# Routing between two mixture layers: comparisons four tiles ahead of their products, the held layer's steps moved up, and fifteen idle products

## The chip, the cores and the metric

The kernel runs on one core of one Trainium2 chip. The metric is the device time of one execution in microseconds. A core has five engines that run their own instruction queues in order: PE (matrix products), DVE (vector), ACT (activation and copies), POOL (GpSimd, which also issues the gathers and scatters) and SP (which issues the plain loads).

## The reference

The reference is an attention layer, then a mixture of 8 experts (each token goes to its best expert, in order of arrival), then a second mixture of 8 experts with a global greedy assignment. The change touches the assignment of the second one:

```python
def _moe2_ref(x, w_gate, w1, w2):
    N, D = x.shape                    # 1152, 512
    E = w_gate.shape[1]               # 8
    cap = N // E                      # 144
    logits = x @ w_gate
    flat = logits.flatten()
    order = np.argsort(-flat)         # all pairs of token and expert, best first
    assigned = -np.ones(N, dtype=np.int64)
    counts = np.zeros(E, dtype=np.int64)
    for idx in order:
        tok, e = (int(idx) // E, int(idx) % E)
        if assigned[tok] >= 0 or counts[e] >= cap:
            continue
        assigned[tok] = e
        counts[e] += 1
    ...
    for e in range(E):
        mask = assigned == e
        h = np.maximum(x[mask] @ w1[e], 0.0)      # w1: 512 x 1024
        out[mask] = h @ w2[e]                     # w2: 1024 x 512
```

## The kernel before

Everything runs in the order in which the program writes it down, engine by engine; nothing is reordered. Tokens lie in 9 tiles of 128.

**The assignment** runs in eight phases. In a phase each token names its best open expert (`Bo`, a one-hot row), and its rank is the number of tokens with the same choice and a larger logit. For that, the maxima of all tokens stand in a row on every partition (`rowb`), `compare(t)` writes `g`, 128 x 1152 ones and zeros for tile t (on DVE; for three of the nine tiles on ACT, as a sign), and `products(g, t)` adds nine products of `g` with `Bo` into one PSUM tile `pc`. Tokens of rank below 144 are placed, and at least one expert is full; its number (`evi`) is what SP needs to load that expert's weights, its token numbers (`tok`) are what POOL needs to gather its rows. The first phase covers nine tiles; the later seven cover the tokens that are left (five tiles: `pos` says where each goes, nine comparisons `cm` and 45 products move the logits there, split in three bf16 parts `S3`), and they are woven into the second mixture's experts.

**The held layer.** The last expert of the first mixture has its second layer held back as filler: `held_steps` yields 24 steps. Steps 1 to 8 and 11 to 18 are six matmuls each, 9 and 19 an ACT eviction of `y`, 10 and 20 a DVE one, 21 and 23 eight transposes, 22 and 24 an ACT copy (to `xo`, to `x2f`) and a scatter of 68 rows into `x2d`, issued by POOL. `fill()` takes the next word of the string FILL and makes as many steps as it has letters f (r: those of the expert before). The first gather of the second mixture reads `x2d`, so it waits for the last scatter.

**Weights of the second mixture** stream from memory in parts of 512 KB, four for each matrix, issued by SP in a fixed order: four of w1 and four of w2 of the first expert, then of the second, and so on. `known(p)` makes SP wait for `evi` of phase p; `quota` says how many parts may go before SP must wait for `passed(n)`, which holds it until POOL has issued the gather and then allows n more. Each w1 part passes through ACT (`wh`, the fp16 half) and DVE (`wl`, the rest).

The lines that set the order around the change:

```python
    for k, t in enumerate(tiles):          # 0 2 1 3 5 4 6 8 7
        g = compare(t)
        if k == 0:
            head(True)
        products(g, t)
        fill()
...
    quota[0] = 3
    known(0)
...
    xg = {0: gather(tok[:, 0])}
    passed(9)
```

Of the kernel before, what the change touches and what calls it, by code (L numbers as in the profile page):

```python
# [9 lines left out]
F32 = mybir.dt.float32  # L10
# [11 lines left out]
def tile_attention_moe_moe(ctx: ExitStack, tc: tile.TileContext, q, k, v, s, wg1, w1a, w2a, capacity,  # L22
                           wg2, w1b, w2b, out, dbg=None):
    nc = tc.nc
# [5 lines left out]
    P = 128  # L30
# [7 lines left out]
    NTT = NTOK // P  # L38
# [6 lines left out]
    C0, C1 = max(CAPS), min(CAPS) // 16 * 16  # L45
# [9 lines left out]
    ident = const.tile([P, P], F16, name="ident")  # L55
# [23 lines left out]
    WSP = [tuple(wsp0.tile([P, 4096], t, name=f"{n}{i}") for n, t in (("wh", F16), ("wl", BF16))) for i in range(2)]  # L79
    WS = {}  # L80

    FILL = ". rf rrrf ffff ff ffff ff ff ff . ff ff ff . . ."

# [6 lines left out]
    HELD = (E - 1,)  # L92

    ONE = (E - 2, E - 1)


    order = {}
# [5 lines left out]
    quota = [99]  # L103
# [1167 lines left out]

    fills = FILL.split()

    def fill():
        for c in fills.pop(0):
            next(todo[c], None)
# [157 lines left out]
    def slot_pe(O, R, n):  # L1434
        for t in range(n):
            nc.tensor.matmul(pt, O[:, t], R[:, t].rearrange("p e h -> p (e h)"), start=t == 0, stop=t == n - 1)
# [119 lines left out]
        nc.vector.tensor_copy(tokl, tok[:, E - 1])  # L1556


    def ranks(pc, m, Bo, Bh, n, act_t):


        order = [t for t in range(n) if t not in act_t]
        for k, t in enumerate(act_t):
            order.insert(min(3 * k + 2, len(order)), t)

        def head(first):
            for t in act_t:
                nc.tensor.matmul(pc, ones, Bh[:, t, None, :].to_broadcast([P, n, E]), start=first,
                                 stop=False, skip_group_check=True)
                nc.tensor.matmul(pc[:, t], negi, Bh[:, t], start=False, stop=False, skip_group_check=True)  # L1570
                first = False

        def compare(t):
            g = gp.tile([P, NTT, P], F16, name="g")[:, :n]
            if t in act_t:
                nc.scalar.activation(g, rowb[:, :n], AF.Sign, bias=m[:, t:t + 1], scale=-1.0)
            else:
                nc.vector.tensor_scalar(g, rowb[:, :n], m[:, t:t + 1], None, op0=OP.is_lt)
            return g

        def products(g, t):
            rhs = Bh if t in act_t else Bo
            for i in range(n):
                nc.tensor.matmul(pc[:, i], g[:, i], rhs[:, t], start=False,
                                 stop=t == order[-1] and i == n - 1, skip_group_check=True)
        return head, order, compare, products
# [23 lines left out]
    def pop_lo():  # L1610
        if late:
            split_lo(*late.pop(0))
# [12 lines left out]
    def choose(p, f):  # L1625
# [5 lines left out]
            lambda: nc.vector.reduce_sum(s2, sel.rearrange("p e h -> p h e"), axis=AX.X),  # L1631
            lambda: nc.vector.tensor_scalar(tok[:, p], s2, float(NTOK - 1), None, op0=OP.min)]

    iotac = iotat[:, :CT * P]
    m, Bo = m0, Bo0
    S3 = rp.tile([P, 3, NTT, E + 1], BF16, name="S3")
    sres = rp.tile([P, 2, NTT, E + 1], F32, name="sres")
    p0 = Banks("A2").tile([P, 512], F32)
    pc = p0[:, :NTT * E].rearrange("p (t e) -> p t e", e=E)
    head, tiles, compare, products = ranks(pc, m, Bo, Bh0, NTT, (1, 4, 7))  # L1640
    for k, t in enumerate(tiles):
        g = compare(t)
        if k == 0:
            head(True)
        products(g, t)
        fill()
    nc.gpsimd.tensor_copy(S3[:, 0], L2T)
    nc.gpsimd.tensor_sub(sres[:, 0], L2T, S3[:, 0])
    nc.gpsimd.tensor_copy(S3[:, 1], sres[:, 0])
    nc.gpsimd.tensor_sub(S3[:, 2], sres[:, 0], S3[:, 1])  # L1650
    mx = rw.tile([P, NTT], F32, name="mx0")
    nc.vector.reduce_max(mx, pc, axis=AX.X)
    BA0 = rw.tile([P, NTT, E], F16, name="BA0")
# [11 lines left out]
    f0, ops = newly_full(0)  # L1665
    O0, R0, places = slot_ones(r0, BA0, L2T[:, :, E], NTT, 0)
    in_turn(ops, places[:3])
    quota[0] = 3
    known(0)
    in_turn(places[3:])  # L1670
    pp = p0[:, 80:80 + NTT]
# [1 line left out]
    for t in range(NTT - 1):  # L1673
        nc.tensor.matmul(pp[:, t + 1:], ones, left[:, t:t + 1].to_broadcast([P, NTT - 1 - t]),
                         start=False, stop=t == NTT - 2, skip_group_check=True)
    fill()
    slot_pe(O0, R0, NTT)
    fill()
    pos = rw.tile([P, NTT], F32, name="pos")
    nc.vector.scalar_tensor_tensor(pos, pp, 1.0, left, op0=OP.add, op1=OP.mult)  # L1680
# [237 lines left out]
    FIRST, THEN = (x.split() for x in (FIRST, THEN))  # L1918
    next(work)
    pop_lo()  # L1920
    XT1[0] = spread(xg.pop(0))
    next(work)
    next(work)
# [62 lines left out]
```

## Time and profile before

| | |
|---|---|
| median of 3 runs (their range) | 463.65 us (463.37 to 463.76) |
| the profiled execution | 468.03 us |
| its span, first to last instruction | 466.2 us |
| mean granted clock of PE, share of full speed | 0.934 |
| PE busy | 402.9 us, 86% |
| DVE, ACT, POOL busy | 308.9, 249.1, 189.9 us |
| moved by DMA | 103.02 MB, mean 221 GB/s |

The profile is one execution; all points in time ("at 292.40") are microseconds from the start of its span. Its own time is 1.8 us over its span, and 4.4 us over the median of the runs, so what the trace shows of waits need not hold to the microsecond in the other executions.

### The profile page before, as it was taken

Reading aid. Unit: us, or ns where it says so; the run is one execution under the profiler, and the core shown is the slowest. Engines: PE = TensorE matmul, PEld = TensorE weight load, DVE = VectorE, ACT = ScalarE, POOL = GpSimd, SP = SyncE. Lnnn points to the kernel's source line nnn. Section 1 sums busy time; section 2 is a strip of 40 time slices with the busy share of each in tenths; the row PEclk is TensorE's granted clock in tenths of the full one; section 3 lists DMA queues with packets and bytes.
Section 4 is the critical chain, followed back from the end, with each engine's and each line's share of the span. In section 5 each row is a group of like instructions: output and inputs, shape, how many; then the busy total and the mean of one; then the engine's idle time right before and its main releaser. Section 6 shows DMA issues by size and latency. Waiting matters only on the chain. (4 is left out here: it accounts for less than half of the span.)

```text
span 466.2 us, 13648 instructions
## 1 busy us (share of the span) xinstructions
PE 402.9 (86%) x5245; PEld 376.6 (81%) x5245; DVE 308.9 (66%) x926; ACT 249.1 (53%) x459; POOL 189.9 (41%) x306
## 2 busy tenths in 40 slices
PE   2679999978979979999999996469989999999970
PEld 1457888867768969999999996459979999999970
DVE  6879999887585557777888944757754664555100
ACT  4447888845752545555668434242746465465320
POOL 4487888858804220410441811422331342342110
PEclk9869999989999998999999989559989999999995
DMA  6797999849834799999996900479996869798000
GB/s 158 173 199 165 215 223 215 190 155 321 265 101 180 200 353 400 346 353 321 296 348 118 167 7 23 160 200 307 364 376 208 284 224 318 255 286 290 29 20 25
DMA packets 94398, 103.02 MB, mean 221 GB/s; under 512 B 56136, under 2 KB 63304, under 8 KB 94323
## 3 DMA queue, kind: packets, MB, share of 16 engines
q1 hardware_dynamic: 88931, 91.85, 68.1%
q0 software_dynamic: 4192, 9.91, 7.0%
q8 instruction: 43, 0.70, 0.6%
q10 hardware_dynamic: 1200, 0.30, 0.3%
q14 instruction: 32, 0.26, 0.2%
HBM read 81.42 MB, written 14.59 MB: 206 GB/s over the span
## 5 line engine op out<-in xcount | busy, mean ns | idle before, releaser
L162 DVE TENSOR_TENSOR wl<-wf,wh 128x1024 bf16<-128x1024 f32 x64 | 77.7, 1234 | 23.3 <-ACT wh L158 23.1
L158 ACT ACTIVATE wh<-wf 128x1024 f16<-128x1024 f32 x64 | 65.7, 1050 | 19.6 <-DMA wf<-in_moe_w_dram 19.6
L986 PE MATMUL C<-h,wf 128*128 128x160 f32 (+7 forms) x544 | 60.3, 273 | 2.2 <-ACT h L940 2.2
L929 PE MATMUL A<-xt,wh 128*128 128x144 f16 (+4 forms) x288 | 60.9, 235 | 0.0
L930 PE MATMUL A<-xt,wh 128*128 128x144 f16 (+4 forms) x288 | 60.9, 235 | 0.0
L931 PE MATMUL A<-xt,wl 128*128 128x144 f16 (+4 forms) x288 | 60.8, 235 | 0.0
L1099 POOL DMA_INDIRECT x2d<-xo,tix x14 | 22.9, 1637 | 86.4 <-DVE l L1095 34.7
L930 PEld LDWEIGHTS <-wh 128*128 128x128 f16 x512 | 51.3, 100 | 1.1 <-issue 0.6
L931 PEld LDWEIGHTS <-wl 128*128 128x128 bf16 x512 | 51.5, 101 | 0.4 <-DVE wl L162 0.4
L929 PEld LDWEIGHTS <-wh 128*128 128x128 f16 x512 | 51.4, 100 | 0.2 <-issue 0.2
L534 ACT ACTIVATE pf<-pE,XB 128x512 f32<-128x512 f32 (+4 forms) x80 | 36.8, 514 | 10.1 <-PE pE L529 9.8
L1860 POOL DMA_INDIRECT out_dram<-x2f,tok x14 | 15.5, 1108 | 64.8 <-ACT h L940 37.3
L986 PEld LDWEIGHTS C<-h,wf 128*128 128x128 f32 x256 | 37.2, 195 | 2.5 <-ACT h L940 2.5
L1840 PE MATMUL C<-h,wf 128*128 128x144 f32 x256 | 37.0, 298 | 2.2 <-ACT h L940 2.2
L412 POOL TENSOR_TENSOR pl<-pf,ph 128x512 f16<-128x512 f32 x30 | 35.5, 1193 | 6.2 <-DVE ph L401 4.0
L486 DVE CUSTOM_DVE_ANT_0 junk<-pM,cb 128x128 f16<-128x128 f32 (+4 forms) x80 | 32.1, 430 | 6.9 <-PE pM L476 6.2
L1840 PEld LDWEIGHTS C<-h,wf 128*128 128x128 f32 x256 | 34.0, 198 | 2.4 <-ACT h L940 2.4
L474 PE MATMUL pM<-al,ar 128*128 128x128 f16 (+2 forms) x96 | 27.8, 328 | 7.0 <-DVE rm L486 7.0
L1441 POOL DMA_INDIRECT xg<-x2d,tok x16 | 22.7, 1418 | 23.6 <-PE C L1840 6.8
L557 PE MATMUL pog<-vf,pf 128*128 128x65 f32 x180 | 28.7, 282 | 0.0
L931 PE MATMUL C<-xt,wl 128*128 128x144 f16 x128 | 25.6, 232 | 0.3 <-DVE wl L162 0.3
L929 PE MATMUL C<-xt,wh 128*128 128x144 f16 x128 | 25.7, 232 | 0.0
(408 smaller groups left out, 1164.9 us busy)
## 6 DMA issues: line engine op xcount, KB each, us to landing
wf<-in_moe_w_dram SPq DMA_DIRECT2D x128, 512.0 KB, 8.7
xd<-zero SPq DMA_DIRECT2D x18, 257.0 KB, 4.7
cb<-cumd SPq DMA_DIRECT2D x16, 288.0 KB, 4.8
x2d<-zero SPq DMA_DIRECT2D x9, 260.5 KB, 4.5
kf<-in_k_dram SPq DMA_DIRECT2D x16, 128.0 KB, 3.7
vf<-in_v_dram SPq DMA_DIRECT2D x16, 128.0 KB, 3.0
qf<-in_q_dram SPq DMA_DIRECT2D x14, 128.0 KB, 2.9
bl<-al SPq DMA_DIRECT2D x16, 72.0 KB, 4.9
```

What stands on the lines that cost most here:

```text
L158: nc.scalar.activation(hi, src, AF.Copy)
L162: nc.vector.tensor_sub(lo, src, hi)
L412: (nc.gpsimd if ENG[name][i % 2] == "P" else nc.vector).tensor_sub(o, x, y)
L474: nc.tensor.matmul(o, AR[m][:, t * P:(t + 1) * P], AL[m][:, j0:j1], start=True, stop=not diag)
L486: nc.vector.tensor_tensor_reduce(junk[:w, :j1 - j0], o, CB[m][:w, j0:j1], 1.0, r if t == 4 and j0 == 0 else -3e38, OP.add, OP.max, r)
L534: nc.scalar.activation(d, o, AF.Exp, bias=x, scale=2.0 ** -13)
L557: nc.tensor.matmul(o, pf[:, c:c + P], VF[n % 4][:, j, h], start=False, stop=j == t)
L929: nc.tensor.matmul(ph[:, g], wh[:, c, fs], xt[:, c], start=c == 0, stop=False)
L930: nc.tensor.matmul(ph[:, g], wh[:, c, fs], xt[:, 4 + c], start=False, stop=False)
L931: nc.tensor.matmul(ph[:, g], wl[:, c, fs], xt[:, c], start=False, stop=c == 3)
L986: nc.tensor.matmul(py[:, g], a[:, f, d], b[:, f], start=k == 0, stop=k == len(terms) - 1)
L1840: nc.tensor.matmul(py[:, g], a[:, f, d], b[:, f], start=k == 0, stop=k == len(terms) - 1)
```

## The change

It makes five edits. (1) In the first phase the comparisons of four tiles stand ahead of the first product, and each later one ahead of the products four tiles before it; the tiles come in the order 0 1 2 4 3 7 5 6 8, so that ACT and DVE take turns. (2) FILL has other words: the held matmuls come within the first three tiles, the second scatter after the eighth. (3) The three-part split of the logits (`S3`, four POOL instructions) stands ahead of the first phase's products instead of behind them. (4) `quota` is 2, not 3. (5) `warm(n)` issues n products of 128 x 512 into a spare bank whose result nobody reads: 6 after the counts of phase 0, 5 after the products with `O0`, 4 ahead of the first `spread`.

```diff
-    FILL = ". rf rrrf ffff ff ffff ff ff ff . ff ff ff . . ."
+    FILL = ". rf rrrf ffff ffffff ffff ffff . . ff ff . . . . ."
+    WARM2 = (6, 5, 4)
...
-    def ranks(pc, m, Bo, Bh, n, act_t):
+    def ranks(pc, m, Bo, Bh, n, act_t, apart=3):
...
-            order.insert(min(3 * k + 2, len(order)), t)
+            order.insert(min(apart * k + apart - 1, len(order)), t)
...
+    def warm(n):
+
+        o = Banks("C1").tile([P, 512], F32)
+        for _ in range(n):
+            nc.tensor.matmul(o, ident, iotat[:, :512], start=True, stop=True)
...
-    head, tiles, compare, products = ranks(pc, m, Bo, Bh0, NTT, (1, 4, 7))
-    for k, t in enumerate(tiles):
-        g = compare(t)
-        if k == 0:
-            head(True)
-        products(g, t)
-        fill()
+    head, tiles, compare, products = ranks(pc, m, Bo, Bh0, NTT, (1, 4, 7), 2)
     nc.gpsimd.tensor_copy(S3[:, 0], L2T)
     nc.gpsimd.tensor_sub(sres[:, 0], L2T, S3[:, 0])
     nc.gpsimd.tensor_copy(S3[:, 1], sres[:, 0])
     nc.gpsimd.tensor_sub(S3[:, 2], sres[:, 0], S3[:, 1])
+    AHEAD = 4
+    gs_ = [compare(t) for t in tiles[:AHEAD]]
+    head(True)
+    for k, t in enumerate(tiles):
+        if k + AHEAD < NTT:
+            gs_.append(compare(tiles[k + AHEAD]))
+        products(gs_[k], t)
+        fill()
...
-    quota[0] = 3
+    quota[0] = 2
...
     fill()
+    warm(WARM2[0])
     slot_pe(O0, R0, NTT)
+    warm(WARM2[1])
     fill()
...
     pop_lo()
+    warm(WARM2[2])
     XT1[0] = spread(xg.pop(0))
```

On DVE, in the first phase, from the first comparison to the maximum over the finished counts (`g` comparisons, `y` the two evictions of the held layer, `mx` the maximum), the rows before:

```order
L1578 TENSOR_SCALAR g<-rowb,m_3109 128x1152 x2
L1253 SCALAR_TENSOR_TENSOR y<-C_5152,y 128x2x136
L1578 TENSOR_SCALAR g<-rowb,m_3109 128x1152 x3
L1253 SCALAR_TENSOR_TENSOR y<-C_5321,y 128x2x136
L1578 TENSOR_SCALAR g<-rowb,m_3109 128x1152
L1652 TENSOR_REDUCE mx_5485<-A_5278 128x9
```

and now:

```order
L1580 TENSOR_SCALAR g<-rowb,m_3109 128x1152 x3
L1255 SCALAR_TENSOR_TENSOR y<-C_5152,y 128x2x136
L1580 TENSOR_SCALAR g<-rowb,m_3109 128x1152
L1255 SCALAR_TENSOR_TENSOR y<-C_5322,y 128x2x136
L1580 TENSOR_SCALAR g<-rowb,m_3109 128x1152 x2
L1662 TENSOR_REDUCE mx_5485<-A_5278 128x9
```

Both evictions stay, one comparison moved ahead of the first and one behind the second.

On POOL, from the last held scatters to the first gather (`S` and `sres` the logits' parts, `xo` and `x2f` the rows of the two scatters), before:

```order
L1099 DMA x2d<-xo,tix 1152x521
L1268 MEMSET x2f 68x8
L1098 TENSOR_SCALAR x2f<-gs 68x1
L1099 DMA x2d<-x2f,tix 1152x521
L1647 CAST S_5276<-L2T 128x81
L1648 TENSOR_TENSOR sres<-L2T,S_5276 128x81
L1649 CAST S_5276<-sres 128x81
L1650 TENSOR_TENSOR S_5276<-sres,S_5276 128x81
L1441 DMA xg<-x2d,tok 72x521 x2
```

and now:

```order
L1649 CAST S_5276<-L2T 128x81
L1650 TENSOR_TENSOR sres<-L2T,S_5276 128x81
L1651 CAST S_5276<-sres 128x81
L1652 TENSOR_TENSOR S_5276<-sres,S_5276 128x81
L1270 MEMSET xo 68x8
L1100 TENSOR_SCALAR xo<-gs 68x1
L1101 DMA x2d<-xo,tix 1152x521
L1270 MEMSET x2f 68x8
L1100 TENSOR_SCALAR x2f<-gs 68x1
L1101 DMA x2d<-x2f,tix 1152x521
L1443 DMA xg<-x2d,tok 72x521 x2
```

The four rows of the parts went from behind the scatters to ahead of them; the gather now follows the second scatter directly.

On SP, where the first expert's w1 is loaded (`evi` the wait for its number, `wf_78` the buffer, `gone` the wait for the gather), before:

```order
L1615 TENSOR_LOAD evi
L1615 ISA x2
L126 ISA
L126 DMA wf_78<-in_moe_w_dram 128x4x256
L126 ISA
L126 DMA wf_78<-in_moe_w_dram 128x4x256
L126 ISA
L126 DMA wf_78<-in_moe_w_dram 128x4x256
L1621 TENSOR_LOAD gone
L1621 ISA x2
L126 ISA
L126 DMA wf_78<-in_moe_w_dram 128x4x256
```

and now:

```order
L1617 TENSOR_LOAD evi
L1617 ISA x2
L128 ISA
L128 DMA wf_78<-in_moe_w_dram 128x4x256
L128 ISA
L128 DMA wf_78<-in_moe_w_dram 128x4x256
L1623 TENSOR_LOAD gone
L1623 ISA x2
L128 ISA
L128 DMA wf_78<-in_moe_w_dram 128x4x256
L128 ISA
L128 DMA wf_78<-in_moe_w_dram 128x4x256
```

The third part went behind the wait for the gather. Since `passed` still allows nine parts, the last part of the second expert's w1 went behind the next such wait in the same way.

## Rows read from the trace of the kernel before

**Rows 1.** Stages: us, busy us of PE, PEld, DVE, ACT, POOL; clock; DMA; GB/s.

```profile
293.00:302.00 9.00, 3.37 (x75) 3.00 (x73) 6.92 (x37) 2.08 (x2) 3.77 (x6) 0.50 0.61 196
320.00:340.00 20.00, 19.69 (x277) 19.42 (x276) 14.47 (x63) 10.09 (x18) 5.97 (x9) 1.00 1.03 339
340.00:344.00 4.00, 1.85 (x15) 1.62 (x14) 2.12 (x8) 2.96 (x5) 0.73 (x1) 0.88 1.05 394
```

**Rows 2.** POOL in time: start, length, operation, idle time before it and its releaser.

```profile
291.66 1.14 POOL L1099 DMA_INDIRECT x2d<-xo,tix  x1 [9.62 <-ACT xo L1267]
295.22 1.13 POOL L1099 DMA_INDIRECT x2d<-x2f,tix  x1 [2.09 <-DVE R L1422]
...
297.16 1.54 POOL L1649 CAST S<-sres 128x81 bf16<-128x81 f32 x1
...
302.94 1.54 POOL L1441 DMA_INDIRECT xg<-x2d,tok  x1 [3.83 <-DVE Bh L1728]
```

**Rows 3.** Issue to landing, us, of the two scatters at 291.66 and 295.22.

```profile
x2d<-xo,tix POOLq DMA_INDIRECT x1, 4.4
x2d<-x2f,tix POOLq DMA_INDIRECT x1, 6.8
```

**Rows 4.** DVE in time, from the first comparison to the logits' move.

```profile
280.42 1.55 DVE L1578 TENSOR_SCALAR g<-rowb,m 128x1152 f16<-128x1152 f32 x2 [1.38 <-ACT rowb L1146]
...
287.58 0.44 DVE L1253 SCALAR_TENSOR_TENSOR y<-C,y 128x272 f16<-128x272 f32 x1 [2.08 <-ACT y L1251]
...
292.40 0.23 DVE L1652 TENSOR_REDUCE mx<-A 128x9 f32<-128x72 f32 x1 [3.65 <-PE A L1584]
...
294.09 0.15 DVE L1596 TENSOR_SCALAR evi<-evf 128x1 int32<-128x1 f32 x1
...
296.72 0.17 DVE L1632 TENSOR_SCALAR tok<-s 72x2 int32<-72x2 f32 x1
...
297.03 1.55 DVE L1696 TENSOR_SCALAR g<-iotat,pos 128x640 bf16<-128x640 f16 x5
```

**Rows 5.** PE in time: held matmuls, one tile's products, and the second mixture's first.

```profile
281.54 0.87 PE L1247 MATMUL C<-h,wf 128*128 128x136 f16 x12
282.25 0.37 PE L1584 MATMUL A<-Bo,g 128*128 128x8 f16 x9
282.48 0.87 PE L1247 MATMUL C<-h,wf 128*128 128x136 f16 x12
...
309.21 0.28 PE L929 MATMUL D<-xt,wh 128*128 128x144 f16 x1 [0.49 <-ACT xt L1464]
```

**Rows 6.** ACT in time: the second eviction of `y`, and the copy ahead of the first scatter.

```profile
287.15 0.40 ACT L1251 ACTIVATE y<-C 128x272 f16<-128x272 f32 x1 [1.92 <-PE C L1247]
...
289.74 1.02 ACT L1267 ACTIVATE xo<-D 68x1024 f16<-68x1024 f16 x1 [2.20 <-PE D L1265]
```

**Rows 7.** SP's queue in time: issues of weight parts, each of 512 KB.

```profile
295.32 0.40 SPq L126 DMA_DIRECT2D wf<-in_moe_w_dram  x1
...
306.75 0.38 SPq L126 DMA_DIRECT2D wf<-in_moe_w_dram  x1
...
317.23 0.33 SPq L126 DMA_DIRECT2D wf<-in_moe_w_dram  x1
```

**Rows 8.** DVE and PE in the first expert's first layer.

```profile
315.25 2.35 DVE L162 TENSOR_TENSOR wl<-wf,wh 128x1024 bf16<-128x1024 f32 x2
...
316.53 0.24 PE L931 MATMUL C<-xt,wl 128*128 128x144 f16 x1 [0.26 <-DVE wl L162]
```

**Rows 9.** ACT and PE in the second expert, where weights are waited for.

```profile
326.20 1.06 ACT L158 ACTIVATE wh<-wf 128x1024 f16<-128x1024 f32 x1 [4.92 <-DMA wf<-in_moe_w_dram]
330.30 0.23 PE L929 MATMUL C<-xt,wh 128*128 128x144 f16 x1
...
341.05 1.06 ACT L158 ACTIVATE wh<-wf 128x1024 f16<-128x1024 f32 x1 [4.36 <-DMA wf<-in_moe_w_dram]
342.45 0.79 PE L1840 MATMUL C<-h,wf 128*128 128x144 f32 x4 [2.15 <-ACT h L940]
```

## The prediction

> **What bounds the kernel now.** I read the stages first. Over most of the span PE is full, as from 320 to 340, where it works 19.69 of 20 us [rows 1]; only around the first routing phase it is empty, with 3.37 us of work in the 9 us from 293 to 302 at half the clock (0.50 granted, that is 1.2 GHz). So I followed what releases what from the first comparison to the second mixture's first matmul at 309.21 [rows 5]. The weights come next, since DMA is full from 320 to 340 (share 1.03, 339 GB/s) [rows 1].
>
> The chain, back from 309.21: the rows of the first expert come from a gather that POOL issues at 302.94 [rows 2], 6.27 us before the first matmul. Its token numbers had been there since 296.72 + 0.17 = 296.89 [rows 4]. What it waited for is the last held scatter, since it reads the same buffer: issued at 295.22 [rows 2], landed after 6.8 us [rows 3], at 302.02; POOL goes on 0.92 later. (The trace names a DVE instruction as releaser; a scatter's landing fits, and the program has POOL wait for it.) The first scatter landed in 4.4 us; the second shared the memory with three weight parts that SP began to issue at 295.32 [rows 3, 7]. So the first 6 us after `tok` are the price of a late scatter, not of routing.
>
> Why is it late? The scatter's rows come from the held layer, which stands between the tiles' products. DVE does the second eviction of `y` at 287.58, having done one comparison after another ahead of it, and the last tiles' products wait for comparisons again: `mx`, which needs them all, starts at 292.40 after 3.65 us of idleness on DVE [rows 4].
>
> **The change, part by part.** *Comparisons ahead, held layer early.* From 281.54 on PE does, by the new order, two more tiles' products and the 60 held matmuls that are left before it needs an eviction. Twelve held matmuls take 0.71 us (281.54 to 282.25) and a tile's products 0.23 (282.25 to 282.48) [rows 5]: 5 x 0.71 + 2 x 0.23 = 4.0, so 285.6. The comparisons don't hold this up: DVE needs 0.78 each [rows 4], starts at 280.42, and has three done by 282.8, while ACT makes tiles 1 and 4. ACT's eviction follows in 0.2 and takes 0.40, DVE's begins 0.43 after ACT's begins (287.15 and 287.58) and takes 0.44 [rows 4, 6]: done at 286.7. Eight transposes, 0.45 by the twelve above, and ACT copies `xo` from 287.1 to 288.1; now it starts at 289.74 [rows 6]. POOL's scatter began 0.90 after that copy's end (290.76 to 291.66) [rows 2, 6], so the first is issued at 289.0. The second copy follows without a gap (1.02 more), and POOL is busy 1.14 with the first scatter and some 0.8 (my allowance) with two small instructions: 290.1 if nothing but the copy counts, 291.0 with POOL; I take 291.0, 4.2 earlier than 295.22. The last two comparisons follow the eviction on DVE: 286.7 + 2 x 0.78 = 288.2, a last product 0.23, so `mx` at 288.5, 3.9 earlier.
>
> *S3 ahead.* These four run on POOL while it waits for `xo`. One of them took 1.54 [rows 2] and they stood between scatter and gather, but the gather waited longer than that, so moving them alone is worth nothing. They do release the 45 products of the logits' move earlier, which no longer reach 302.
>
> *The scatter's landing.* SP's issue follows `evi` by 1.23 (294.09 to 295.32) [rows 4, 7]; both move with `mx`, so the first part is issued at 291.4, right after the scatter as now, but two parts instead of three. The landing lies between the 4.4 of the undisturbed scatter and the 6.8 of the disturbed one: 295.4 to 297.8. I take 6.0, since two thirds of the disturbance are there for as long as the scatter runs: 297.0, and the gather at 297.9. Earlier by 5.0; bounds 4.2 and 6.6.
>
> *Gather to first matmul:* 6.27 as before, so 304.2, 5.0 earlier. POOL may be slowed there. The Trainium skill, "SBUF — State Buffer", section "Who interferes with whom", says that a vector instruction in a two-port mode blocks GpSimd for its whole length, descriptor generation included. The trace agrees for POOL's arithmetic: the cast of 1.54 us at 297.16 lasted as long as five comparisons of 1.55 at 297.03 [rows 2, 4]. By that rule a gather among such comparisons would lose up to 1.5 us. In my sum the nine comparisons are over by then (they start 3.9 earlier, or 2.9 if the idle products run slow), so I charge nothing and keep 1.5 for the range.
>
> *Idle products.* The six stand in a wait of PE for DVE, the five in front of the logits' move, the four in front of the transposes that wait for the gather. No trace row shows one; 512 columns against the 136 of a held matmul (0.71 / 12 = 0.059 us) give 0.22 us each, 0.44 at half clock: 1.3 to 2.7, 1.1 to 2.2 and 0.9 to 1.8 us. `tok` may be late by 1 us through the first, and still precedes the landing by 3. So they cost nothing as long as the scatter ends last. Do they give anything? A faster PE in the first expert's layer 1 doesn't: the third quarter's `wl` is the first of two splits of 2.35 us that begin at 315.25, 6 us after the first matmul, and DVE is busy throughout; PE already waits 0.26 for it at 316.53 [rows 8]. I take 0.
>
> *Quota 2.* One more part comes behind the gather. The stream proper now begins at 306.75 [rows 7], 3.81 after the gather; it will begin at 301.7, 5.0 earlier, with 0.52 MB more to bring: 1.6 us at 339 GB/s [rows 1]. Also the second expert's last w1 part goes behind the second gather; now it is issued at 317.23 [rows 7], then at about 317 (12.9 us after the first matmul, where the next parts are issued now): the stream has just run dry there, some 0.4 us lost.
>
> *What is late next.* In the second expert PE waits 2.15 us at 342.45, because ACT stands 4.36 us at 341.05 for the third expert's w1 and has an eviction of `h` queued behind it [rows 9]. This wait ends by the stream. The stream gains 5.0 - 1.6 - 0.4 = 3.0, PE 5.0: so PE waits 4.1 there and leaves 3.0 us earlier. Behind it PE is full to the end, and everything shifts.
>
> The sum: 468.03 - 3.0 = 465.0 against the profiled execution; carried over as a difference, 463.65 - 3.0 = 460.6. That the profiled execution is 4.4 above the median leaves open whether the stream is as tight in the others; part of the wait may be missing there, which gives up to 2 us more. I take 460.3.
>
> **The rivals.** *The whole gain arrives.* The stream keeps up (no or a shorter wait at 342.45 in unprofiled runs), or the scatter lands undisturbed (gather 6.6 earlier, of which the stream leaves 4.6): 463.65 - 4.6 or - 5.0, so 458.6 to 459.0, both together 457. For it: the 4.4 us between profile and median, and two parts instead of three. Against it: DMA at a share of 1.03.
>
> *The scatter is hardly faster, or the gather is blocked.* 4.2 - 1.6 - 0.4 = 2.2, less up to 1.5 for the blocked gather: 461.4 to 463.0. For it: the parts still go out within half a microsecond of the scatter.
>
> *The clock.* By rows, PE's clock was 0.88 over the 4 us with that 2.15 us wait, so it fell behind it [rows 1, 9]. If the idle products lift the clock for layer 1, its first half ends in about half of the 7.3 us from 309.21 to 316.53 [rows 5, 8], and PE stands some 3.6 us for `wl`, with a fall behind it that costs 1 to 2 us. That is an estimate; PE is 2.0 ahead of the stream, which takes up most of it: 460.3 to 461. The Trainium skill, "TensorE: Matmul & The Clock Gate", section "Why this matters for your kernels", says that idle gaps between bursts send the clock back to 1.2 GHz. By that rule the edit would fill one gap and open another; the trace agrees with the fall, and the time would stay as above.
>
> *Slower: the part behind the second gather.* Now ACT gets the second expert's w1 at 326.20 and PE needs it at 330.30; hi and lo splits take 1.06 and 1.2, so 1.8 us are spare [rows 9]. The part issued at 317.23 took 9.0 to 326.2. Issued at 317 it decides once it needs over 11.1 us; at 13, 466 or so. Against it: less is queued ahead of it than now, so I expect 5 to 6.
>
> **How the numbers follow.** My forecast (459.2 to 461.4) gets 0.5, the whole gain (below 459.2) 0.27, the small one (461.4 to 463.0, with some beyond) 0.18, slower 0.05. A measurement of this kernel can tell 0.2%, 0.93 us. Of the small gain a third lies within it, and of the slower case a little: faster 0.88, same 0.08, slower 0.04. The range takes in the whole gain down to 457.6 and the small one up to 462.7.
>
> **What would show it.** `mx` 3.9 us earlier than 292.40; the second scatter near 291 and its landing in about 6 us; the gather near 298, first matmul near 304; a wait of PE in the second expert of 3 to 4 us instead of 2.15. It would be wrong if the gather stayed near 302, if the idle products stood between `tok` and anything that ends last, or if w1 of the second expert came after 328.

## The result and the profile after

The changed kernel takes 456.39 us (median of 4 runs, 455.61 to 464.24) against 463.51 us of the kernel before beside it (4 runs, 461.79 to 463.76): a ratio of 0.9849, 95% interval 0.9815 to 0.9882. Now and then a run falls into a slower state, here the one of 464.24; such runs count in the medians, but not in the ratios, here and below. That is 7.1 us less. The forecast was 460.3, which is 3.35 less than the 463.65 that it started from, and 456.39 lies below the range's 457.6.

| | before | after |
|---|---|---|
| the profiled execution, us | 468.03 | 456.74 |
| its span, us | 466.2 | 454.7 |
| mean granted clock | 0.934 | 0.970 |

The two profiled executions are 11.5 us of span apart, and not all of it is the change's. The first tile's products, the first work that the change moves, start at 281.30 before and at 276.78 after: 4.52 us lie ahead of the change. In unchanged code from 20 to 30 us the granted clock was 0.50 before and 0.72 after, from 260 to 280 it was 0.91 and 1.00. So from here on points in time count from the first tile's products, written as +x. The offset is 281.30 for the groups of rows of before, 276.78 for the rows below.

| us behind the first products | before | after | earlier by | forecast |
|---|---|---|---|---|
| `mx` | +11.10 | +7.23 | 3.9 | 3.9 |
| second held scatter issued | +13.92 | +9.50 | 4.4 | 4.2 |
| gather issued | +21.64 | +16.03 | 5.6 | 5.0 |
| first matmul of the second mixture | +27.91 | +21.80 | 6.1 | 5.0 |
| SP's first weight part behind the second gather | +40.84 | +34.74 | 6.1 | 5.0 |
| ACT gets the third expert's w1 | +59.75 | +54.35 | 5.4 | 3.0 |
| PE's wait in the second expert ends | +61.15 | +55.76 | 5.4 | 3.0 |
| end of the span | +184.9 | +177.9 | 7.0 | 3.0 |

PE of the changed kernel in time (start, length, operation, idle time before it and its releaser), to be read against [rows 5, 9]:

```profile
276.78 0.38 PE L1586 MATMUL A<-Bo,g 128*128 128x8 f16 x9
277.01 1.58 PE L1249 MATMUL C<-h,wf 128*128 128x136 f16 x24
...
285.06 1.45 PE L1640 MATMUL C<-iotat,ident 128*128 128x512 f16 x6
...
287.57 1.24 PE L1640 MATMUL C<-iotat,ident 128*128 128x512 f16 x5
288.94 2.66 PE L1710 MATMUL A<-S,g 128*128 128x27 bf16 x45
...
293.06 1.03 PE L1640 MATMUL C<-iotat,ident 128*128 128x512 f16 x4
...
298.58 0.28 PE L931 MATMUL D<-xt,wh 128*128 128x144 f16 x1 [0.49 <-ACT xt L1466]
...
332.54 0.76 PE L1852 MATMUL C<-h,wf 128*128 128x144 f32 x4 [1.97 <-ACT h L942]
```

The held matmuls are done in bursts of 24, 24 and 12, and among the nine tiles' products PE stands for a comparison only once, 0.27 us. Before, it stood three times, and the eight transposes that each scatter needs come behind such a product:

```profile
284.13 0.38 PE L1584 MATMUL A<-Bh,g 128*128 128x8 f16 x9 [0.79 <-ACT g L1576]
...
288.80 0.38 PE L1584 MATMUL A<-Bo,g 128*128 128x8 f16 x9 [1.26 <-DVE g L1578]
289.04 0.61 PE L1265 MATMUL D<-ident,y 128*68 128x128 f16 x8
291.96 0.40 PE L1584 MATMUL A<-Bh,g 128*128 128x8 f16 x9 [2.30 <-ACT g L1576]
292.22 1.05 PE L1265 MATMUL D<-ident,y 128*68 128x128 f16 x8
```

```profile
290.66 1.24 ACT L1576 ACTIVATE g<-rowb,m 128x1152 f16<-128x1152 f32 x1
```

The longest of these waits, 2.30 us, is for ACT's last comparison, which stood behind ACT's copy of `xo` at 289.74 [rows 6].

The fifteen idle products (line 1640) take 1.45, 1.24 and 1.03 us, 0.24 to 0.26 each where the estimate was 0.22, and end 4.5 us ahead of the matmul at 298.58. The wait in the second expert is 1.97 us, not the 4.1 forecast.

DVE in time, against [rows 4]:

```profile
275.90 2.28 DVE L1580 TENSOR_SCALAR g<-rowb,m 128x1152 f16<-128x1152 f32 x3 [1.38 <-ACT rowb L1148]
...
281.64 0.44 DVE L1255 SCALAR_TENSOR_TENSOR y<-C,y 128x272 f16<-128x272 f32 x1 [1.86 <-ACT y L1253]
282.00 1.54 DVE L1580 TENSOR_SCALAR g<-rowb,m 128x1152 f16<-128x1152 f32 x2
284.01 0.23 DVE L1662 TENSOR_REDUCE mx<-A 128x9 f32<-128x72 f32 x1 [0.47 <-PE A L1586]
...
286.02 0.82 DVE L1430 TENSOR_TENSOR O<-iota0f,hq 128x648 f16<-128x648 f32 x1
...
288.51 2.74 DVE L1708 TENSOR_SCALAR g<-iotat,pos 128x640 bf16<-128x640 f16 x9
```

Three comparisons stand ahead of everything, two behind the second `y`, and DVE is idle 0.47 us ahead of `mx`, where it was 3.65. The nine comparisons of the logits' move end at 291.25.

POOL in time, against [rows 2], and behind it issue to landing of the two scatters, against [rows 3]:

```profile
284.45 1.18 POOL L1101 DMA_INDIRECT x2d<-xo,tix  x1 [4.57 <-ACT x2f L1269]
...
286.28 1.55 POOL L1101 DMA_INDIRECT x2d<-x2f,tix  x1 [0.31 <-POOL x2f L1100]
292.81 1.06 POOL L1443 DMA_INDIRECT xg<-x2d,tok  x1 [4.98 <-DVE Bo L1739]
294.18 1.02 POOL L1443 DMA_INDIRECT xg<-x2d,tok  x1 [0.30 <-issue]
```

```profile
x2d<-xo,tix POOLq DMA_INDIRECT x1, 4.4
x2d<-x2f,tix POOLq DMA_INDIRECT x1, 5.7
```

The second scatter lands at 286.28 + 5.7 = 291.98, and the gather follows 0.83 later: the same wait as before, shorter by an earlier start and by 1.1 us of landing. The first gather takes 1.06 us where it took 1.54.

ACT in time, against [rows 9]:

```profile
316.81 1.06 ACT L160 ACTIVATE wh<-wf 128x1024 f16<-128x1024 f32 x1 [6.15 <-DMA wf<-in_moe_w_dram]
...
331.13 1.06 ACT L160 ACTIVATE wh<-wf 128x1024 f16<-128x1024 f32 x1 [4.17 <-DMA wf<-in_moe_w_dram]
```

Stages of the changed kernel, columns as in [rows 1]: first the stretch that answers to 293 to 302, then the first expert's first layer, then the wait in the second expert, which was at 340 to 344:

```profile
288.50:297.50 9.00, 5.18 (x66) 3.12 (x65) 5.36 (x21) 2.77 (x4) 2.32 (x5) 1.00 0.56 165
297.50:304.50 7.00, 6.51 (x87) 6.40 (x88) 6.27 (x30) 4.50 (x6) 0.49 (x2) 0.52 1.10 321
330.00:334.00 4.00, 2.04 (x20) 1.81 (x19) 2.44 (x11) 2.87 (x5) 0.64 (x1) 1.00 1.04 381
332.00:336.00 4.00, 3.46 (x31) 3.45 (x32) 3.64 (x7) 3.40 (x7) 1.80 (x2) 1.00 1.05 399
```

The clock is 1.00 through the first stretch (0.50 before, at rows 1's 293 to 302), but the first layer runs at 0.52 again, since PE stands for the gather first. Around the wait it stays 1.00; before it was 0.88, and 0.69 in the four us behind:

```profile
309.00:316.00 7.00, 6.79 (x89) 6.78 (x89) 6.79 (x31) 4.02 (x6) 0.48 (x2) 0.52 1.11 307
344.00:348.00 4.00, 4.00 (x25) 4.00 (x25) 2.61 (x5) 1.75 (x4) 2.77 (x3) 0.69 1.02 379
```

These two stages are of the kernel before: its first layer at 0.52 too, and the fall behind its wait.

### The profile page after: what moved, and what is told of

It is laid out like the page before. It is cut to its first block, busy times and chain, and to the rows that moved or that the text cites. A ratio compares the mean times of both kernels' runs of the same rounds, so it can differ in the third digit from the quotient of the medians.

```text
span 454.7 us, 13676 instructions
## 1 busy us (share of the span) xinstructions
PE 400.4 (88%) x5260; PEld 371.6 (82%) x5260; DVE 309.2 (68%) x926; ACT 249.1 (55%) x459; POOL 190.9 (42%) x306
## 5 line engine op out<-in xcount | busy, mean ns | idle before, releaser
L988 PE MATMUL C<-h,wf 128*128 128x160 f32 (+7 forms) x544 | 58.6, 269 | 1.7 <-ACT h L942 1.7
L933 PE MATMUL A<-xt,wl 128*128 128x144 f16 (+4 forms) x288 | 59.5, 231 | 0.0
L931 PE MATMUL A<-xt,wh 128*128 128x144 f16 (+4 forms) x288 | 59.5, 231 | 0.0
L932 PE MATMUL A<-xt,wh 128*128 128x144 f16 (+4 forms) x288 | 59.5, 231 | 0.0
L1101 POOL DMA_INDIRECT x2d<-xo,tix x14 | 23.0, 1640 | 78.0 <-DVE l L1097 40.2
L932 PEld LDWEIGHTS <-wh 128*128 128x128 f16 x512 | 50.7, 99 | 1.1 <-issue 0.6
L931 PEld LDWEIGHTS <-wh 128*128 128x128 f16 x512 | 50.8, 99 | 0.2 <-issue 0.2
L988 PEld LDWEIGHTS C<-h,wf 128*128 128x128 f32 x256 | 36.2, 190 | 1.9 <-ACT h L942 1.9
L1852 PE MATMUL C<-h,wf 128*128 128x144 f32 x256 | 35.5, 290 | 2.0 <-ACT h L942 2.0
L1852 PEld LDWEIGHTS C<-h,wf 128*128 128x128 f32 x256 | 32.5, 190 | 2.2 <-ACT h L942 2.2
```

Of the source, the lines that this page charges most:

```text
L931: nc.tensor.matmul(ph[:, g], wh[:, c, fs], xt[:, c], start=c == 0, stop=False)
L932: nc.tensor.matmul(ph[:, g], wh[:, c, fs], xt[:, 4 + c], start=False, stop=False)
L933: nc.tensor.matmul(ph[:, g], wl[:, c, fs], xt[:, c], start=False, stop=c == 3)
L988: nc.tensor.matmul(py[:, g], a[:, f, d], b[:, f], start=k == 0, stop=k == len(terms) - 1)
L1852: nc.tensor.matmul(py[:, g], a[:, f, d], b[:, f], start=k == 0, stop=k == len(terms) - 1)
```

## The experiments

Each was timed in rounds beside the kernel before on the same chip. Ratios are to that, with the 95% interval. The points behind the first products are from each run's trace; "end" is the end of the span. The last column is SP's first weight part behind the second gather, of which more below.

| run | median us (before) | ratio | second scatter | gather | first matmul | third w1 at ACT | end | SP |
|---|---|---|---|---|---|---|---|---|
| e5_order_only | 460.54 (466.59) | 0.9864 [0.982, 0.9908] | +9.48 | +16.10 | +22.00 | +52.8 | +176.5 | +34.9 |
| e3_old_order | 463.5 (464.39) | 0.9977 [0.9947, 1.0007] | +14.02 | +21.47 | +27.24 | +59.3 | +182.9 | +40.2 |
| e6_idle_only | 466.69 (466.59) | 0.9992 [0.9954, 1.0031] | +13.93 | +21.36 | +27.42 | +57.7 | +182.6 | +40.3 |
| e1_no_idle | 457.45 (464.39) | 0.9847 [0.9799, 0.9896] | +9.50 | +16.07 | +21.78 | +52.8 | +176.3 | +34.7 |
| e4_quota2_only | 464.56 (464.39) | 1.0043 [1.0003, 1.0084] | +13.92 | +21.39 | +27.85 | +57.6 | +182.2 | +40.8 |
| e2_quota3 | 457.61 (464.39) | 0.9861 [0.9812, 0.9911] | +9.51 | +16.12 | +21.72 | +52.1 | +175.7 | +34.6 |
| e8_passed10 | 460.92 (466.59) | 0.989 [0.9843, 0.9937] | +9.51 | +16.06 | +21.63 | +52.0 | +176.9 | +34.5 |
| e7_quota0 | 468.05 (466.59) | 1.0014 [0.9983, 1.0044] | +9.50 | +15.10 | +26.62 | +58.2 | +183.7 | +39.6 |
| e17_quota1 | 462.37 (463.16) | 0.9987 [0.9958, 1.0016] | +9.51 | +15.89 | +26.83 | +58.0 | +181.5 | +39.8 |
| e10_ahead_oldfill | 460.44 (465.09) | 0.9914 [0.9886, 0.9943] | +10.58 | +17.21 | +22.83 | +53.1 | +176.7 | +35.8 |
| e16_ahead_oldfill | 459.67 (463.16) | 0.9932 [0.9902, 0.9961] | +10.69 | +17.49 | +23.14 | +54.3 | +177.9 | +36.1 |
| e11_fill_only | 463.88 (465.09) | 0.9978 [0.9954, 1.0001] | +12.84 | +17.97 | +25.82 | +56.7 | +180.4 | +38.8 |
| e12_before_less | 465.48 (465.09) | 0.9993 [0.9969, 1.0018] | +13.93 | +21.28 | +27.88 | +58.0 | +181.7 | +40.8 |
| e13_after_less | 460.65 (465.09) | 0.9926 [0.9899, 0.9953] | +9.51 | +15.96 | +21.59 | +52.3 | +177.1 | +34.5 |
| e15_after_less | 458.1 (463.16) | 0.9869 [0.982, 0.9919] | +9.50 | +15.99 | +21.56 | +53.0 | +178.2 | +34.5 |
| e14_change | 458.78 (463.16) | 0.9899 [0.9858, 0.994] | +9.50 | +16.06 | +21.70 | +53.5 | +177.0 | +34.7 |

**Which edits bring it.** The kernel before with the new order of comparisons, products and held steps alone (edits 1 and 2; the logits' parts stay behind, `quota` stays 3, no idle products):

```diff
-    FILL = ". rf rrrf ffff ff ffff ff ff ff . ff ff ff . . ."
+    FILL = ". rf rrrf ffff ffffff ffff ffff . . ff ff . . . . ."
...
-    for k, t in enumerate(tiles):
-        g = compare(t)
-        if k == 0:
-            head(True)
-        products(g, t)
+    gs_ = [compare(t) for t in tiles[:AHEAD]]
+    head(True)
+    for k, t in enumerate(tiles):
+        if k + AHEAD < NTT:
+            gs_.append(compare(tiles[k + AHEAD]))
+        products(gs_[k], t)
```

> The kernel before with the new order of the first phase alone (comparisons four ahead, tile order, fill string): three weight parts, the split of the logits behind the loop, no idle products. Theory A: within 0.3% of the whole change, 456 to 458 us. If quota, split and idle products matter together: 459 to 461.

It measured 0.9864, with the same points behind the first products as the whole change. Its counterpart is the changed kernel with that piece turned back:

> The change with the tile loop and the fill string of before; the split of the logits ahead, two parts and the idle products stay. Theory A: nearly the whole gain is gone, 461 to 463 us, since the second scatter is issued near 295 again. Theory B or C: most of the gain stays, 457 to 459.

0.9977, an interval that takes in no change, and the points of the kernel before. The idle products alone in the kernel before (e6: `warm` and its three calls as in the change), and the changed kernel without them (e1):

```diff
-    WARM2 = (6, 5, 4)
+    WARM2 = (0, 0, 0)
```

> The kernel before with the fifteen idle products alone. Theory A: no change, 463 to 465 us, since each stands in a wait. Theory B: 1.5 to 2 us faster, 462 to 463, with the clock at full speed in the logits' move and behind the second expert's wait.

> The change without its fifteen idle products, all else kept. Theory A (the gain comes through the earlier scatter and gather alone): 456 to 457 us, within 0.2% of the whole change; the gather comes 4.5 to 5 us before that of the kernel before, counted from the first tile's products. Theory B (the idle products hold the clock up, and this saves time in the routing and behind the second expert's wait): 1.5 to 2.5 us slower than the change, 458 to 459, and the clock at half in the stretch of the logits' move.

0.9992 and 0.9847: they give and cost nothing that these intervals can show. So edits 1 and 2 bring the gain, and what the other three add can't be told from nothing.

**How it splits between them.** The changed kernel with the old words of FILL, once, and once more beside the changed kernel itself on another chip; then the kernel before with the new words alone (e11, the same line the other way round):

```diff
-    FILL = ". rf rrrf ffff ffffff ffff ffff . . ff ff . . . . ."
+    FILL = ". rf rrrf ffff ff ffff ff ff ff . ff ff ff . . ."
```

> The changed kernel with the old words of FILL: the comparisons stand four tiles ahead, the held layer stays spread over the tiles. If the comparisons carry the gain, PE reaches the second eviction after about 60 x 0.059 + 7 x 0.23 = 5.1 us from its first products, the last scatter follows within 0.6 us of the 9.50 that the whole change has, and the time is within 1 us of it (ratio 0.985 to 0.988 to the kernel before). If the held layer's words carry it, the scatter stays behind 12 us and the ratio is above 0.993.

> The changed kernel with the old words of FILL, beside the changed kernel. Its trace had the first matmul of the second mixture 1.0 us later behind the first products (22.8 against 21.8), so if that instant decides the time, it is 1.0 us above the changed kernel beside it; if the two edits only work together, 3 us or more.

> The kernel before with the new words of FILL alone: the held layer comes within the first three tiles, the comparisons stand where they stood. The eviction of y on DVE then comes ahead of some five comparisons, so I expect the maximum over the counts some 9 us behind the first products (11.10 before, 7.23 with the whole change) and the last scatter near 10.5 us. If the held layer's words carry the gain, the ratio is near 0.988; if the comparisons do, or if both are needed, it is above 0.993.

The comparisons ahead without the new words came to 0.9914, between the 0.988 that the first expectation allowed if they carried all and the 0.993 of the other, and to 0.9932, just above that. The scatter came at +10.58 and +10.69, 1.1 to 1.2 us behind that of the whole change, and not within 0.6. In e16 the time is 0.9 us above the changed kernel beside it by the medians (459.67 against 458.78), 1.5 by the ratios (0.9932 against 0.9899), where the first matmul is 1.4 us later; the intervals overlap. The words alone came to 0.9978, an interval that takes in no change. So the comparisons carry most of the gain, about two thirds to four fifths in e16, and the words give the rest only together with them. My numbers for the words alone were wrong: `mx` came at +12.71, not +9, and the scatter at +12.84, not +10.5. POOL and DVE of e11_fill_only:

```profile
301.08 3.03 POOL L1441 DMA_INDIRECT xg<-x2d,tok  x1 [2.00 <-DVE g L1696]
304.41 1.05 POOL L1441 DMA_INDIRECT xg<-x2d,tok  x1 [0.30 <-issue]
```

```profile
289.13 0.44 DVE L1253 SCALAR_TENSOR_TENSOR y<-C,y 128x272 f16<-128x272 f32 x1 [3.28 <-ACT y L1251]
289.49 3.00 DVE L1578 TENSOR_SCALAR g<-rowb,m 128x1152 f16<-128x1152 f32 x4
...
300.41 2.74 DVE L1696 TENSOR_SCALAR g<-iotat,pos 128x640 bf16<-128x640 f16 x9
```

With the held layer early and no comparisons ahead, DVE stands 3.28 us in front of `y` with four comparisons queued behind it. And since the routing is later too (`tok` is ready at 300.43), the gather at 301.08 falls into the nine comparisons and takes 3.03 us instead of 1.06. That is the rival of the blocked gather, here in full: 2 us. The Trainium skill, "SBUF — State Buffer", section "Who interferes with whom", says that a DVE instruction in a two-port mode shuts GpSimd out for its whole length; this row agrees, with 2.0 us more beside 2.74 us of comparisons.

**Parts ahead of the gather.** `quota` 2 in the kernel before (e4); 3 in the changed kernel (e2); and ten parts instead of nine behind the first gather in the changed kernel (e8), which puts the last part of the second expert's w1 ahead of the second gather again:

```diff
e4
-    quota[0] = 3
+    quota[0] = 2
e2
-    quota[0] = 2
+    quota[0] = 3
e8
-    passed(9)
+    passed(10)
```

> The kernel before with two weight parts ahead of the gather instead of three, nothing else. Theory C: the scatter lands 1 us sooner, gather 1 us sooner, 462 to 463 us. The prediction's term for the stream: 1 to 2 us slower than before, 464.5 to 465.5.

> The change with three weight parts ahead of the gather, as before, instead of two. Theory C (two parts disturb the scatter less, and the later part costs nothing): the scatter takes 6.5 to 7 us to land instead of 5.7, and the time is 0.8 to 1.2 us longer than the change, 457.3. The prediction's own term (the extra part behind the gather costs the weight stream 1.6 to 2.0 us): 0.5 to 1.5 us faster than the change, 455 to 456.

> The change with ten instead of nine parts allowed behind the first gather, so that the second expert's last w1 part is issued with its three others again. If its delay costs anything (the prediction charged 0.4 us): 0.4 us faster than the change, 456.0; if not, the same within what can be told.

With the new order `quota` 3 (0.9861) and 2 (0.9849) can't be told apart, nor 0.989 with ten parts; alone, 2 was 0.4% slower, just outside no change. The part moved behind the second gather costs no time that can be told. Then none and one part ahead of the gather in the changed kernel:

```diff
e7
-    quota[0] = 2
+    quota[0] = 0
...
-    passed(9)
+    passed(11)
e17
-    quota[0] = 2
+    quota[0] = 1
...
-    passed(9)
+    passed(10)
```

> The change with no weight part ahead of the gather, and eleven instead of nine allowed behind it, so that the later waits stand where they stood. Theory C's mechanism by itself: the scatter lands undisturbed after 3.3 to 4.4 us and the gather comes 1.3 to 2.4 us sooner. The prediction's term for the stream: two parts of 1.6 us later, against that 1.3 to 2.4 sooner, so 1 to 2 us slower than the change at the second expert's wait, 457.5 to 458.5; if the stream is not what ends there, 454.5 to 456.

> The changed kernel with one weight part ahead of the gather and ten behind it. If parts in flight slow the scatter's landing (5.7 us behind two of them, 4.4 undisturbed), the gather is issued some 0.5 us earlier behind the first products (15.5 instead of 16.0), and the first matmul with it, if its second to fourth parts come in time: 0.5 us less, too little to be told. If the first expert's own weights are late, as with none ahead, the time rises by 2 us or more.

Both lose nearly all the gain. With none, the gather comes at +15.10, 0.9 earlier; with one, at +15.89, hardly. But the first matmul comes at +26.6 and +26.8. ACT of e17_quota1, and PE's transposes of the gathered rows:

```profile
302.00 1.06 ACT L160 ACTIVATE wh<-wf 128x1024 f16<-128x1024 f32 x1 [6.28 <-DMA wf<-in_moe_w_dram]
302.96 0.75 ACT L1148 ACTIVATE rowb<-A 128x384 f32<-128x384 f32 x2
304.44 0.64 ACT L1466 COPY xt<-A 128x576 f16<-128x576 f16 x1 [0.73 <-PE A L1463]
```

```profile
303.49 1.15 PE L1463 MATMUL A<-ident,xg 72*128 72x72 f16 x16 [7.87 <-ACT rowb L1148]
```

ACT's queue has the splits of two weight parts ahead of its copies to `rowb`; PE's transposes wait for these, and `xt`, which PE needs for its first matmul, is copied behind the transposes. The second part, issued behind the gather, arrives at 302.00, and all of this waits for it. So 2 is the least that this order of ACT's queue allows, and with a third nothing changes that can be told.

**Is the weight stream a limit?** The four loads of the first expert's second matrix (2.1 MB) left out, in the kernel before (e12) and in the changed one (e13, and e15 once more):

```diff
-        nc.sync.dma_start(t[sl], src[sl])
+        if i != 2 * E + 1:
+            nc.sync.dma_start(t[sl], src[sl])
```

> The kernel before without the loads of the first expert's second matrix in the second mixture (its four parts, 2.1 MB; that expert then multiplies with what the buffer held, so its rows are not the reference's). At 339 GB/s the stream behind it comes some 6 us earlier. If the stream sets the end in the second expert, as the prediction had it, the wait of 2.15 us there goes, with the fall of the clock behind it: 2 to 4 us less than before. If the stream is no limit, under 1 us.

> The changed kernel with the same loads left out. By the prediction PE waits 4.1 us for the stream there, so it would gain 4 us or more over the changed kernel, more than the kernel before gains, and stand 5 us or more below it with the loads left out. If the stream is no limit in either, both gain under 1 us, and the two without these loads differ by the same 6 to 7 us as the two with them.

The first moved nothing: 0.9993, interval 0.9969 to 1.0018, where 2 to 4 us less would have been 0.991 to 0.996. The second stood at 0.9926, 4.8 us below the first, which neither theory had quite, and without the changed kernel on its chip. So both were timed together, with the changed kernel unaltered:

> The changed kernel once more, unaltered, on the chip on which the next three are timed, since the two runs with a matrix left out were timed where the change itself was not. 0.985 to 0.990 to the kernel before.

> The changed kernel without the loads of the first expert's second matrix in the second mixture (its rows are then not the reference's). If PE waits for the weight stream in the changed kernel's second expert, as the prediction had it, 3 to 4 us below the changed kernel beside it; if the stream is no limit, the same within 1 us.

458.78 and 458.10: without 2.1 MB 0.7 us less by the medians and 1.4 by the ratios (0.9899 and 0.9869), with overlapping intervals. That lies between the two expectations and by itself decides nothing. The kernel before does decide, and so do the traces: without these loads PE still waits in the second expert, 1.02 us in e13 and 1.80 in e15, against 1.97 and 0.71 with them (the changed kernel's two traces). These bytes are no limit, though ACT still waits for weights. ACT of e15_after_less, and what SP's queue waited for from 313 to 318 (total, times, longest):

```profile
335.60 1.06 ACT L161 ACTIVATE wh<-wf 128x1024 f16<-128x1024 f32 x1 [4.00 <-DMA wf<-in_moe_w_dram]
```

```profile
SPq L1624 <- POOL gone L1623: 4.3, 1, 4.3
```

The third expert's w1 comes at 335.60 - 282.56 = +53.0 (+52.3 in e13) against +53.5 with all loads, where the bytes left out are worth 2.1 MB / 339 GB/s = 6.2 us [rows 1]. What takes these 6.2 us up is a stop: SP stands for the second gather, and the third expert's w1 is issued behind it. The same wait in the kernel before (320 to 322) and in the changed one (309 to 312), each with the issue behind it:

```profile
SPq L1621 <- POOL gone L1620: 3.8, 1, 3.8
322.14 0.39 SPq L126 DMA_DIRECT2D wf<-in_moe_w_dram  x1
```

```profile
SPq L1623 <- POOL gone L1622: 3.7, 1, 3.7
311.52 0.34 SPq L128 DMA_DIRECT2D wf<-in_moe_w_dram  x1
```

322.14 is 12.93 us behind the first matmul at 309.21, and 311.52 is 12.94 behind 298.58. In all eighteen traces, with the old order or the new, none to three parts ahead of the first gather, and the 2.1 MB loaded or not, that distance is 12.86 to 12.95 us, while the wait itself is 2.4 to 4.3 us long. What comes behind the stop was not varied: up to the last part of the third expert's w1 SP issues eight parts there, nine in the changed kernel, in stages whose DMA share is 1.05 [rows 1] and 1.04. No run left out any of these.

## Why the prediction was wrong

**What held.** The chain did: the gather waits for the second held scatter. In e3 and e16 the trace names that scatter's landing as the releaser. POOL of e16_ahead_oldfill:

```profile
296.55 1.06 POOL L1443 DMA_INDIRECT xg<-x2d,tok  x1 [5.68 <-DMA x2d<-x2f,tix]
```

`mx` came 3.9 us earlier as forecast, the scatter 4.4 (4.2). The logits' parts and the idle products were costed at nothing, and e5_order_only is 0.9864 without either. The gather was not blocked, as the nine comparisons were over by then. The reading of why the scatter was late was half right: DVE, whose row of comparisons the prediction names first, was idle for 2.08 us ahead of its eviction [rows 4]. It was PE that stood for comparisons, longest for the last one on ACT.

**Small terms.** The landing took 5.7 us, not 6.0, but not for the reason given, so that 6.0 was near is luck. The prediction counted on two parts disturbing the scatter less than three. With the first part issued 0.1 us behind the scatter, two parts gave 6.6 us (e3, e4) and three 6.8 (before); in the new order the gather came at +16.12 with three (e2) and at +16.03 to +16.07 with two. What changed is that the first part went out 1.5 us behind the scatter at 286.28, and not 0.4:

```profile
287.75 0.40 SPq L128 DMA_DIRECT2D wf<-in_moe_w_dram  x1
```

With one part ahead the gather came only 0.1 to 0.2 us earlier than with two or three, with none 0.9 to 1.0. Gather to first matmul shrank from 6.27 to 5.77: the first gather took 1.06 us instead of 1.54, since in the old order it meets a `wl` split of DVE (the last section has the rows). So the first matmul came 6.1 earlier in this pair of traces instead of 5.0. In the other executions of the old order with all loads (e3, e4, e6: +27.24 to +27.85) against the new with the same words and at least two parts (+21.63 to +22.00) it is 5.2 to 6.2.

**The step that failed** is "What is late next": "The stream gains 5.0 - 1.6 - 0.4 = 3.0, PE 5.0: so PE waits 4.1 there and leaves 3.0 us earlier." I had the stream run from the first gather on at 339 GB/s, so that one more part behind that gather shifts everything behind it. It doesn't: SP stops at the second gather, for 3.7 us in the trace after and 4.3 with 2.1 MB less to bring. The third expert's w1 is issued behind that stop, and the stop ends 12.9 us behind the first matmul, so it moves with PE. The prediction had this distance (it wrote "12.9 us after the first matmul, where the next parts are issued now") and counted it as 0.4 us lost rather than as the place from which the stream starts again. Of the extra part's 1.6 us, now ahead of the third w1, 0.7 were left in this pair: ACT's wait ends 54.35 - 34.74 = 19.6 us behind the stop, 18.9 before. In the other traces with all loads this distance is 16.8 to 19.2 us with two parts ahead of the first gather and 17.3 to 17.9 with three, so even the 0.7 can't be told from what executions differ by. PE's wait ends 5.4 us earlier, not 3.0, and it is 1.97 us long, not 4.1.

**The wait itself** was no property of the order. Old order: 2.15 us in the trace of before, 1.0 in e3, 0.6 in e6, none to be seen in e4. New order: 2.0, 1.1 (e5), 0.7 (e2), 0.7 (e14), none to be seen in e1 and e8. I built on one execution, 4.4 us above the median, in which the clock fell behind that wait (0.88, then 0.69). Two traces of the new order have the same fall, e7 behind a wait of 1.84 us and e15 behind 1.80, and the changed kernel has none behind 1.97. The four us that begin 1.5 us behind the wait, in e7, e15 and the changed kernel:

```profile
345.30:349.30 4.00, 4.00 (x26) 4.00 (x24) 2.74 (x6) 1.76 (x4) 2.65 (x3) 0.70 1.04 407
```

```profile
338.50:342.50 4.00, 4.00 (x24) 4.00 (x23) 2.53 (x5) 1.73 (x4) 2.85 (x3) 0.66 1.03 406
```

```profile
334.00:338.00 4.00, 4.00 (x39) 3.98 (x38) 2.56 (x5) 2.09 (x5) 2.85 (x3) 1.00 1.03 404
```

From the end of this wait to the end of the span it is 123.8 to 124.1 us in the three traces with the fall. In the others that wait there it is 122.1 to 122.3, but for e6 and e13 (123.5 and 123.3), where PE waits once more, 1.3 and 1.0 us. So the fall accounts for the last 1.6 us of the 7.0 in the pair of traces, and it goes with the execution and not with the order.

The ends of the spans of e3, e4 and e6 are +182.2 to +182.9, mean 182.6; those of the changed kernel, e14, e1, e2, e5 and e8 are +175.7 to +177.9, mean 176.7. So 5.8 us is what the order gives from the first products on (6.4 with the trace of before counted too), about what the first matmul gains. From the first matmul to the end of the span it is 153.8 to 157.0 us in all eighteen traces, with the old order (153.8 to 157.0) as with the new (153.9 to 157.0): within that spread nothing behind the first matmul takes the gain back. The medians of these kernels, each against the kernel before on its chip, lie 4.4 to 7.1 us lower. The 7.1 of the first comparison is at the upper end of that; what is between them may be in part the clock in code ahead of the change, where the first products start anywhere from 276.8 to 285.7 us. How much is that was not measured by itself.

**The rivals.** "The whole gain arrives", at 0.27, came nearest, by its first half: the first matmul's gain passes through whole. Its ground, that the stream keeps up, was not quite what happened, since ACT still waits 4.17 us for weights, and its own figures, 458.6 to 459.0 or 457 with both halves, lie above 456.39. "The clock" was wrong in its premise: in the changed kernel the idle products hold 1.00 (2.4 GHz) through the logits' move, but the first layer runs at 0.52 either way, and e1 and e6 show no time in it. "The part behind the second gather" did not come as a slower kernel, but the traces have a little of it: ACT gets the second expert's w1 316.81 - 298.58 = 18.2 us behind the first matmul, 17.0 before, and PE waits for `xt`, which stands behind its splits on ACT, 0.4 us in the changed kernel's first trace, 1.1 in e1, 0.9 in e14, and in the old order 0.9 in e3 and 0.8 in e4. All these have the part moved (four more that have it moved, e10, e13, e15 and e16, don't wait), and no trace with it in its old place shows more than 0.2.

## What to carry to other kernels

When a gain passes into a stream of loads, look for the waits that stop the stream: behind a stop, the loads move with whatever ends it, and here 2.1 MB ahead of it cost nothing that could be told. Leaving out some of the loads tells whether their bytes cost time; to price a wait for loads, those between the last stop and the wait would have to go, which was not done here. Where the trace is one execution well off the median, a wait of 2 us in it is no base for a term until a second execution shows it. Work moved early on one engine (here the held layer) gives little unless what is queued behind its eviction on the next engine moves too.

## What the hardware did that was not expected

A gather of 72 rows took 1.06 us alone and 3.03 us beside nine comparisons of 2.74 us in all. A single TENSOR_TENSOR holds it up as well. In the old order the first gather begins while DVE does a `wl` split, 128 x 1024 numbers in 1.22 us. POOL and DVE of e12_before_less:

```profile
304.86 1.90 POOL L1442 DMA_INDIRECT xg<-x2d,tok  x1 [3.46 <-DVE Bh L1729]
```

```profile
304.59 1.22 DVE L163 TENSOR_TENSOR wl<-wf,wh 128x1024 bf16<-128x1024 f32 x1
```

| | e3 | e6 | before | e4 | e12 |
|---|---|---|---|---|---|
| split and gather under way together, us | 0.19 | 0.56 | 0.58 | 0.83 | 0.94 |
| the gather, us | 1.12 | 1.52 | 1.54 | 1.78 | 1.90 |
| its end behind the end of the split, us | 0.93 | 0.95 | 0.95 | 0.95 | 0.95 |

In the twelve traces of the comparisons ahead, where it meets no split, it takes 1.06 to 1.08 us. So it ends about 0.95 us behind the split, whenever it began, and the 3.03 us end 0.96 behind the ninth comparison (304.11 and 303.15). Scatters show the same beside `O` (a TENSOR_TENSOR of 0.82 us): in the changed kernel the second one meets it and takes 1.55 us, the first 1.18; in e10 and e16 the first meets it and takes 1.74, the second 1.12. The lengths of POOL's rows are rough, and no run took the split or `O` away; that they hold the issue up is read from these neighbours.

The undisturbed landing of a scatter of 68 rows is 4.4 us in both kernels, but the second one landed in 5.7 us where the first weight part followed 1.5 us behind its issue. What stretches it beyond the parts in flight stays open: in e16 the first scatter, 1.0 us ahead of the first part, landed in 6.8 us, and the second, 1.4 behind that part, in 5.9.
